# Start of a fused attention and MoE kernel: half of the first weight block in fp32, half cast on arrival, transposes moved, tiny loads dropped

## Chip, cores, metric

The kernel runs on one core of a Trainium2 chip. The metric is device time in microseconds (us) of one execution, lower is better. The time before the change is 219.72 us, the median of 5 runs (219.17 to 220.25).

## What is computed

The reference has two stages. The first is a two-way cross attention between `x` (8 batches, 8 heads, 512 rows, 64 wide) and `state` (8 batches, 8 heads, 32 rows, 64 wide). The second is a two-layer MLP with SiLU on all 4352 rows of its result.

```python
scores = scale * x @ state.T          # (B, H, 512, 32)
a      = softmax(scores)
xread  = a @ state                    # 512 rows per batch and head
a2     = softmax(scale * state @ x.T)
sread  = a2 @ x                       # 32 rows per batch and head
attn   = concat([xread, sread], axis=2)       # rows of 8 heads * 64 = 512
h      = attn @ w_in                  # 512 -> 2048
out    = (h * sigmoid(h)) @ w_out     # 2048 -> 512
```

## The kernel before, in words

The work goes batch by batch. For a batch `b`, TensorE transposes `x` (`x_T`, line 140), multiplies by the state to get the scores (`sc`), ScalarE takes the exponential (`ex`), VectorE and GpSimd normalise (`red`, `rec`, `norm_m`, `norm_g`), and TensorE transposes the softmax weights (`a_T`, line 223) into the tile `aT`. The first MLP layer is not applied to `xread`: since `xread @ w_in` equals `a @ (state @ w_in)`, the kernel forms `W1 = state @ w_in` once per batch (`w1_m`, line 275, in four column blocks `j` of 512, with `w1_e` casting each block from PSUM into the tile `W1`). Then `g1(b, ft)` (line 313) multiplies a 128-column piece of `W1` by `aT` for two halves and ScalarE applies SiLU to the sum; `g2` (line 339) multiplies the result by `w_out`, and `G2(b, ft)` does so for the four row tiles of one `ft`. `sread_m`, `sread_n`, `sread_t` compute the `sread` rows. `st_T(b)` transposes the state of a batch into `sbd`, which `w1_m` uses as its stationary operand.

The whole order of every engine is written out by hand (a manual schedule). Until line 572 the start is one long list; from line 575 on, a table of steps (`plan`) places the work of the later batches between the `g2` matmuls. The change touches the start only.

In the start, before the change:

- SyncE (its queue of transfers) loads `x` of batch 0 in four pieces (line 378), the state of batch 1 (`st_f[1]`, line 379), the first column block of `w_in` in four fp32 pieces `w_f[:, kt]` (line 381), then a part of `w_out` as fp32 `wo_f` (line 437). ScalarE's queue loads `st_f[0]` and two tiny pieces `tch` (lines 375 and 376, 0.5 KB each), GpSimd's queue a third (line 383). The other weights and `x` of batches 1 and 2 are loaded through GpSimd's queue, some with a cast on the way (`load_wi`, `load_wo`, `load_x`).
- Matmuls on a tile of zeros (`warm`, line 365) stand in TensorE's order at several places; `warm(6, "o0", 512)` (line 477) is the last group ahead of the first weight block.
- The first block of `W1` of batch 0 comes from fp32 operands: `w1f_m` (line 290) multiplies the fp32 state `sbd_f` by the four pieces of `w_f` (8 matmuls). After it come half of the evictions (`w1_e`, 256 columns, both by ScalarE), then `a_T` with both halves copied by VectorE, then the other evictions (lines 478 to 481).
- The bf16 copy of that block in `w_in_sb`, which batch 1 needs, is made by VectorE in four casts, two ahead of `sread_n` and two after the cast of the state of batch 1 (lines 493 to 500).

Of the kernel before, what the change touches and what calls it, by code (L numbers as in the profile page):

```python
# [8 lines left out]
FP32 = mybir.dt.float32  # L9
# [10 lines left out]
def kernel(  # L20
# [8 lines left out]
    nc = tc.nc  # L29
    ds = bass.ds  # L30

    B, H, S, NS, D, DM, DF = 8, 8, 512, 32, 64, 512, 2048
    KT = 4
    SCALE = 0.125

    pers = ctx.enter_context(tc.tile_pool(name="pers", bufs=1))
# [3 lines left out]

    zeros = pers.tile([128, 512], BF16, name="zeros")
    ident = pers.tile([128, 128], BF16, name="ident")
    tch = [pers.tile([16, KT, 2], FP32, name=f"tch{i}") for i in range(3)]
    st_f = [pers.tile([128, 128], FP32, name=f"st_f{i}") for i in range(2)]
    w_f = pers.tile([128, KT, 512], FP32, name="w_f")
    wo_f = pers.tile([128, 4, DM], FP32, name="wo_f")
    sbd_f = pers.tile([128, KT, NS], FP32, name="sbd_f")
# [16 lines left out]
    w_in_sb = pers.tile([128, KT, DF], BF16, name="w_in_sb")  # L64
# [3 lines left out]
    bank = {  # L68
        n: psum.tile([128, 512], FP32, name=f"ps_{n}")
        for n in ("o0", "o1", "w0", "w1", "h0", "h1", "a0", "a1")  # L70
    }
# [3 lines left out]
    win_re = moe_w_in.rearrange("(kt p) f -> p kt f", p=128)  # L75
    wout_re = moe_w_out.rearrange("(ft p) m -> p ft m", p=128)

    def bf(name):
        return bank[name][:].bitcast(BF16)

    def cp(eng, dst, src):
        if eng == "dve":
            nc.vector.tensor_copy(dst, src)  # L83
        elif eng == "pool":
            nc.gpsimd.tensor_copy(dst, src)  # L85
        else:
            nc.scalar.activation(dst, src, func=COPY, bias=0.0)  # L87
# [33 lines left out]
    def st_T(b, bk, e0, e1):  # L121
        v = bf(bk)[:, 0:128]
        nc.tensor.transpose(v, st_nat[:, b, :], ident[:])
        for half, e in ((0, e0), (1, e1)):
            cp(
                e,
                sbd[ds(64 * half, 64), b, :, half, :],
                v[ds(64 * half, 64)].rearrange("p (ns kt) -> p kt ns", kt=KT),
            )
# [93 lines left out]
    def a_T(b, bks):  # L223
        n = 2 // len(bks)
        for i, (bk, e) in enumerate(bks):
            v = bf(bk).rearrange("p (h c t) -> p h c t", h=2, c=4)
            for half in range(n):
                for c in range(4):
                    nc.tensor.transpose(
                        v[:, half, c, :], an[b % 2][:, i * n + half, c, :, :], ident[:]  # L230
                    )
            cp(e, aT[b % 2][:, ds(i * n, n)], v[:, ds(0, n)])
# [32 lines left out]
    def sread_t(b, bk, eng):  # L265
        v = bf(bk)[:, 512:640]
        nc.tensor.transpose(v, sr[:], ident[:])
        cp(
            eng,
            xsT[:, :, b // 4, :, b % 4],  # L270
            v.rearrange("p (kt ns) -> p kt ns", kt=KT),
        )


    def w1_m(b, j, bks):
        for kt in range(KT):
            for half in range(2):
                nc.tensor.matmul(  # L278
                    bank[bks[half]][ds(32 * kt, 32), :],
                    sbd[ds(64 * half, 64), b, kt, half, :],  # L280
                    w_in_sb[ds(64 * half, 64), kt, ds(512 * j, 512)],
                    start=True,
                    stop=True,
                    skip_group_check=True,
                    tile_position=(64 * half, 32 * kt),
                )

    def w1f_m(bks):  # L290
        for kt in range(KT):
            for half in range(2):
                nc.tensor.matmul(  # L293
                    bank[bks[half]][ds(32 * kt, 32), :],
                    sbd_f[ds(64 * half, 64), kt, :],
                    w_f[ds(64 * half, 64), kt, :],
                    start=True,
                    stop=True,
                    skip_group_check=True,
                    tile_position=(64 * half, 32 * kt),  # L300
                )

    def w1_e(b, j, bks, engs, c0=0, n=512):
        for half in range(2):
            cp(
                engs[half],
                W1[b % 2][:, half, ds(512 * j + c0, n)],
                bank[bks[half]][:, ds(c0, n)],
            )
# [3 lines left out]
    def g1(b, ft):  # L313
        bk = bank[f"h{hctr[0] % 2}"]
        hctr[0] += 1
        if b < B:
            for half in range(2):
                nc.tensor.matmul(  # L318
                    bk[:],
                    W1[b % 2][:, half, ds(128 * ft, 128)],  # L320
                    aT[b % 2][:, half, :, :],
                    start=(half == 0),
                    stop=(half == 1),
                    skip_group_check=True,
                )
            nc.scalar.activation(g[b % 2][:, ft, :], bk[:], func=SILU, bias=0.0)  # L326
        else:
            for kt in range(KT):
                nc.tensor.matmul(  # L329
                    bk[:, 0:256],  # L330
                    w_in_sb[:, kt, ds(128 * ft, 128)],
                    xsT[:, kt, :, :, :],
                    start=(kt == 0),
                    stop=(kt == KT - 1),
                    skip_group_check=True,
                )
            nc.scalar.activation(g_s[:, ft, :], bk[:, 0:256], func=SILU, bias=0.0)  # L337

    def g2(b, tt, ft, bk, cols=(0, 512)):
        src = g[b % 2] if b < B else g_s  # L340
        c0, c1 = cols
        nc.tensor.matmul(  # L342
            bank[bk][:, c0:c1],
            src[:, ft, ds(128 * tt, 128)],
            w_out_sb[:, ft, c0:c1],
            start=(ft == 0),
            stop=(ft == 15),
            skip_group_check=True,
        )
# [15 lines left out]
    def warm(n, bk, w=128):  # L365
        for i in range(n):
            nc.tensor.matmul(  # L367
                bank[bk][:, 0:w], zeros[:, 0:128], zeros[:, 0:w], start=True, stop=True,
                skip_group_check=True,
            )  # L370

    with tc.manual_schedule():

        nc.scalar.dma_start(st_f[0][:], state[0].rearrange("h ns d -> ns h d"))
        nc.scalar.dma_start(tch[0][:], win_re[0:128:8, :, 0:2])
        nc.scalar.dma_start(tch[1][:], wout_re[0:128:8, 0:4, 0:2])
        for kt in range(KT):
            load_x(0, nc.sync, kt, 1)
        nc.sync.dma_start(st_f[1][:], state[1].rearrange("h ns d -> ns h d"))
        for kt in range(KT):  # L380
            nc.sync.dma_start(w_f[:, kt, :], win_re[:, kt, 0:512])
        make_identity(nc, ident[:])
        nc.gpsimd.dma_start(tch[2][:], win_re[0:128:8, :, 512:514])
        nc.vector.memset(zeros[:], 0.0)
        nc.vector.memset(sbd[:], 0.0)
        for i in range(2):
# [12 lines left out]
        def G2(b, ft):  # L399
            for tt in range(4):  # L400
                g2(b, tt, ft, OB[tt])

        def W1x(b, j, bks, engs):
            w1_m(b, j, bks)
            w1_e(b, j, bks, engs)
# [68 lines left out]
        for i in range(4):  # L474
            cp("pool", w_out_sb[:, i, :], wo_f[:, i, :])
        nc.scalar.preload_act_table(SILU)
        warm(6, "o0", 512)
        w1f_m(("w0", "w1"))
        w1_e(0, 0, ("w0", "w1"), ("act", "act"), 0, 256)
        a_T(0, (("a0", "dve"), ("a1", "dve")))  # L480
        w1_e(0, 0, ("w0", "w1"), ("act", "dve"), 256, 256)
        warm(2, "h1", 512)
        load_x(1, nc.gpsimd, 2, 2)
# [12 lines left out]
        cp("dve", st_nat[:, 1, :], st_f[1][:])  # L496
        g1(0, 2)
        g1(0, 3)
        for kt in range(2, 4):
            cp("dve", w_in_sb[:, kt, 0:512], w_f[:, kt, :])  # L500
        st_T(1, "a0", "dve", "dve")
        G2(0, 0)
        sread_t(0, "a1", "dve")
        G2(0, 1)
        w1_m(1, 0, AB)
        W1x(0, 1, HB, DA)
        w1_e(1, 0, AB, DA)
        G2(0, 2)
        g1(0, 4)
        G2(0, 3)  # L510
        g1(0, 5)
        W1x(1, 1, AB, DD)
        G2(0, 4)
# [80 lines left out]
        def tiled(b, tt):  # L594
            cur, nxt, third, srb = (TB[(tt + i) % 4] for i in range(4))
            bks = ((nxt, third), HB, AB, (cur, srb))
            sread_m(b, srb)
            sread_n(b, srb)
            for j in range(4):
                w1_m(b, j, bks[j])  # L600
            for j in range(4):
                w1_e(b, j, bks[j], ("act", "dve"))
# [93 lines left out]
```

## Time and profile before

| what | value |
|---|---|
| median of 5 runs | 219.72 us (219.17 to 220.25) |
| the profiled execution's own time | 219.44 us |
| its span (first to last instruction) | 217.6 us |
| TensorE matmul busy | 211.2 us, 97% of the span |
| ScalarE, VectorE, GpSimd busy | 134.3 us (62%), 84.6 us (39%), 45.5 us (21%) |
| granted clock of TensorE | 1.000 (mean of the core) |

The span leaves 1.84 us around it (219.44 less 217.6). The busy share of TensorE is an average, and its records overlap because matmuls are pipelined, so a full slice can still hold waits. In the views, a line begins with the start in us and the duration in us, then the engine, the line of the kernel, the operation, the tiles as out<-in, shapes, and in brackets the idle time of the engine ahead of it with what ended it. PE is TensorE's matmuls, PEld its weight loads, DVE VectorE, ACT ScalarE, POOL GpSimd, SPq the transfers that SyncE issues.

### The profile page before, as it was taken

Reading aid. Unit: us, or ns where it says so; the run is one execution under the profiler, and the core shown is the slowest. Engines: PE = TensorE matmul, PEld = TensorE weight load, DVE = VectorE, ACT = ScalarE, POOL = GpSimd, SP = SyncE. Lnnn points to the kernel's source line nnn. Section 1 sums busy time; section 2 is a strip of 40 time slices with the busy share of each in tenths; the row PEclk is TensorE's granted clock in tenths of the full one; section 3 lists DMA queues with packets and bytes.
Section 4 is the critical chain, followed back from the end, with each engine's and each line's share of the span. In section 5 each row is a group of like instructions: output and inputs, shape, how many; then the busy total and the mean of one; then the engine's idle time right before and its main releaser. Section 6 shows DMA issues by size and latency. Waiting matters only on the chain.

```text
span 217.6 us, 4108 instructions
## 1 busy us (share of the span) xinstructions
PE 211.2 (97%) x1664; PEld 104.6 (48%) x1664; DVE 84.6 (39%) x176; ACT 134.3 (62%) x225; POOL 45.5 (21%) x87
## 2 busy tenths in 40 slices
PE   7989999999999999999999999999999999999993
PEld 7633454454444444444444444544454444566553
DVE  3765537832930463147313840276017501111110
ACT  3753485679767947884789458855885586233211
POOL 4596209300700070016001600070001000000000
PEclk9999999999999999999999999999999999999999
DMA  6999995696394149317831695146012311111112
GB/s 184 288 266 257 245 267 90 46 270 210 73 219 166 51 112 246 128 48 122 203 111 50 93 214 179 51 115 148 29 48 42 107 48 48 51 48 48 48 51 96
DMA packets 37555, 27.86 MB, mean 128 GB/s; under 512 B 22176, under 2 KB 31776, under 8 KB 37536
## 3 DMA queue, kind: packets, MB, share of 16 engines
q1 hardware_dynamic: 31280, 21.63, 37.5%
q0 software_dynamic: 5392, 5.44, 12.8%
q10 hardware_dynamic: 864, 0.53, 0.8%
q8 instruction: 13, 0.21, 0.4%
q14 instruction: 6, 0.05, 0.1%
HBM read 17.30 MB, written 8.91 MB: 120 GB/s over the span
## 4 chain that ended last, share of the span: by engine, by line
PE 94%; DVE 3%; ACT 1%; issue 0%; DVEq 0%; ACTq 0%
PE ps_o L342 28%; PE ps_w L342 26%; PE ps_h L318 25%; PE ps_h L329 3%; PE ps_o L367 2%; PE ps_a L175 2%; PE ps_a L278 1%; PE ps_w L293 1%; DVE w_in_sb L83 1%; PE ps_o L278 1%; PE ps_w L278 1%; PE ps_h L278 1%; DVE W L83 1%; PE ps_o L245 1%; DVE xT L83 1%; PE ps_o L143 0%
## 5 line engine op out<-in xcount | busy, mean ns | idle before, releaser
L326 ACT ACTIVATE g<-ps_h 128x512 bf16<-128x512 f32 x128 | 76.0, 597 | 36.6 <-PE ps_h L318 29.9
L318 PE MATMUL ps_h<-aT,W 128*128 128x512 bf16 x256 | 75.8, 379 | 0.2 <-DVE W L83 0.2
L342 PEld LDWEIGHTS <-g 128*128 128x128 bf16 x512 | 49.0, 98 | 54.9 <-issue 2.5
L342 PE MATMUL ps_w<-w_out_sb,g 128*128 128x512 bf16 x256 | 73.3, 379 | 0.0
L342 PE MATMUL ps_o<-w_out_sb,g 128*128 128x512 bf16 x256 | 65.9, 379 | 0.2
L318 PEld LDWEIGHTS <-W 128*128 128x128 bf16 x256 | 24.1, 98 | 28.1 <-issue 1.6
L201 POOL TENSOR_TENSOR an<-en,rs 128x512 bf16<-128x512 bf16 x8 | 8.4, 1054 | 112.3 <-ACT en L186 73.1
L83 DVE COPY o_sb<-ps_w 128x512 f32<-128x512 f32 (+1 forms) x13 | 8.5, 659 | 53.1 <-PE ps_w L342 53.0
L83 DVE COPY o_sb<-ps_o 128x512 f32<-128x512 f32 x14 | 9.5, 686 | 29.6 <-PE ps_o L342 29.5
L85 POOL CAST x_u<-x_f 128x256 bf16<-128x256 f32 x44 | 18.0, 454 | 0.0
L196 DVE TENSOR_REDUCE rs<-en 128x16 f32<-128x512 bf16 x14 | 9.2, 660 | 15.4 <-ACT en L186 15.3
L337 ACT ACTIVATE g_s<-ps_h 128x256 bf16<-128x256 f32 x16 | 6.1, 383 | 14.0 <-PE ps_h L329 14.0
L329 PE MATMUL ps_h<-xsT,w_in_sb 128*128 128x256 bf16 x64 | 9.6, 273 | 0.0
L83 DVE CAST W<-ps_a 128x512 bf16<-128x512 f32 x12 | 8.1, 682 | 3.7 <-PE ps_a L278 3.7
L87 ACT ACTIVATE o_sb<-ps_o 128x512 f32<-128x512 f32 (+1 forms) x4 | 2.2, 544 | 10.7 <-PE ps_o L342 7.9
L186 ACT ACTIVATE en<-ps_a 128x512 bf16<-128x512 f32 (+1 forms) x16 | 8.3, 568 | 0.5 <-PE ps_a L175 0.5
L329 PEld LDWEIGHTS <-w_in_sb 128*128 128x128 bf16 x64 | 6.3, 98 | 4.1
L175 PEld LDWEIGHTS <-xT 128*128 128x128 bf16 x128 | 6.0, 99 | 4.0 <-DVE xT L83 1.0
L186 ACT ACT_TABLE_LOAD x6 | 7.7, 1283 | 0.1
L609 ACT ACT_TABLE_LOAD x6 | 7.7, 1283 | 0.1
L87 ACT ACTIVATE o_sb<-ps_w 128x512 f32<-128x512 f32 (+1 forms) x5 | 2.7, 533 | 8.2 <-issue 6.6
L175 PE MATMUL ps_a<-sbd,xT 128*128 128x64 bf16 x120 | 6.1, 193 | 0.6 <-DVE xT L83 0.6
(87 smaller groups left out, 169.1 us busy)
## 6 DMA issues: line engine op xcount, KB each, us to landing
out_dram<-o_sb SPq DMA_DIRECT2D x32, 256.0 KB, 2.7
x_f<-in_x_dram SPq DMA_DIRECT2D x5, 1024.0 KB, 6.9
w_in_sb<-in_moe_w_in_dram POOLq DMA_DIRECT2D x3, 512.0 KB, 9.6
w_out_sb<-in_moe_w_out_dram POOLq DMA_DIRECT2D x3, 512.0 KB, 10.0
x_f<-in_x_dram SPq DMA_DIRECT2D x4, 256.0 KB, 3.9
w_f<-in_moe_w_in_dram SPq DMA_DIRECT2D x4, 256.0 KB, 5.4
wo_f<-in_moe_w_out_dram SPq DMA_DIRECT2D x4, 256.0 KB, 6.1
x_f<-in_x_dram POOLq DMA_DIRECT2D x2, 512.0 KB, 9.4
```

The lines of the kernel that those rows point to most:

```text
L83: nc.vector.tensor_copy(dst, src)
L85: nc.gpsimd.tensor_copy(dst, src)
L175: nc.tensor.matmul(v[:, kt % 2, :, c, :], xT[b % 2][:, kt, c, :], sbd[:, b, kt, :, :], start=True, stop=True, skip_group_check=True,)
L186: nc.scalar.activation(en[b % 2][:, :, :, ds(kt, n), :].rearrange("p h c k s -> p k (h c) s"), v[:, ds(kt % 2, n)], func=EXP, bias=0.0, sc ...
L196: nc.vector.tensor_reduce(v, en[b % 2][:, :, :, ds(kt, n), :], axis=AX, op=ADD)
L201: e.tensor_tensor(an[b % 2][:, ds(h0, hn), :, ds(kt, n), :].rearrange("p h c k s -> p (h c) k s"), en[b % 2][:, ds(h0, hn), :, ds(kt, n), ...
L278: nc.tensor.matmul(bank[bks[half]][ds(32 * kt, 32), :], sbd[ds(64 * half, 64), b, kt, half, :], w_in_sb[ds(64 * half, 64), kt, ds(512 * j, ...
L318: nc.tensor.matmul(bk[:], W1[b % 2][:, half, ds(128 * ft, 128)], aT[b % 2][:, half, :, :], start=(half == 0), stop=(half == 1), skip_group ...
L326: nc.scalar.activation(g[b % 2][:, ft, :], bk[:], func=SILU, bias=0.0)
L329: nc.tensor.matmul(bk[:, 0:256], w_in_sb[:, kt, ds(128 * ft, 128)], xsT[:, kt, :, :, :], start=(kt == 0), stop=(kt == KT - 1), skip_group_ ...
L342: nc.tensor.matmul(bank[bk][:, c0:c1], src[:, ft, ds(128 * tt, 128)], w_out_sb[:, ft, c0:c1], start=(ft == 0), stop=(ft == 15), skip_group ...
L609: nc.scalar.preload_act_table(SILU)
```

## The change

The three tiny loads and their tiles go. `w1f_m` takes one `kt` and is called for `kt` 0 and 1 only. For `kt` 2 the piece `w_f` is cast to bf16 by ScalarE, for `kt` 3 by VectorE, and `w1_m`, which now takes a list of `kt`, does these two from the bf16 tile. `a_T` stands ahead of those two, and its second half is copied by ScalarE instead of VectorE. The evictions of the first 256 columns are split between ScalarE and VectorE. Five of six zero matmuls ahead of the block go. The later casts of `kt` 2 and 3 go. `G2(0, 2)` moves ahead of the blocks `w1_m(1, 0)` and `W1x(0, 1)`, and `G2(0, 3)` ahead of `g1(0, 4)`.

```diff
-    tch = [pers.tile([16, KT, 2], FP32, name=f"tch{i}") for i in range(3)]
-    def w1_m(b, j, bks):
-        for kt in range(KT):
+    def w1_m(b, j, bks, kts=range(KT)):
+        for kt in kts:
...
-    def w1f_m(bks):
-        for kt in range(KT):
-            for half in range(2):
+    def w1f_m(bks, kt):
+        for half in range(2):
...
         nc.scalar.dma_start(st_f[0][:], state[0].rearrange("h ns d -> ns h d"))
-        nc.scalar.dma_start(tch[0][:], win_re[0:128:8, :, 0:2])
-        nc.scalar.dma_start(tch[1][:], wout_re[0:128:8, 0:4, 0:2])
...
         make_identity(nc, ident[:])
-        nc.gpsimd.dma_start(tch[2][:], win_re[0:128:8, :, 512:514])
...
         nc.scalar.preload_act_table(SILU)
-        warm(6, "o0", 512)
-        w1f_m(("w0", "w1"))
-        w1_e(0, 0, ("w0", "w1"), ("act", "act"), 0, 256)
-        a_T(0, (("a0", "dve"), ("a1", "dve")))
+        warm(1, "o0", 512)
+        w1f_m(("w0", "w1"), 0)
+        w1f_m(("w0", "w1"), 1)
+        cp("act", w_in_sb[:, 2, 0:512], w_f[:, 2, :])
+        cp("dve", w_in_sb[:, 3, 0:512], w_f[:, 3, :])
+        a_T(0, (("a0", "dve"), ("a1", "act")))
+        w1_m(0, 0, ("w0", "w1"), (2, 3))
+        w1_e(0, 0, ("w0", "w1"), ("act", "dve"), 0, 256)
         w1_e(0, 0, ("w0", "w1"), ("act", "dve"), 256, 256)
         warm(2, "h1", 512)
...
         g1(0, 2)
         g1(0, 3)
-        for kt in range(2, 4):
-            cp("dve", w_in_sb[:, kt, 0:512], w_f[:, kt, :])
         st_T(1, "a0", "dve", "dve")
         G2(0, 0)
         sread_t(0, "a1", "dve")
         G2(0, 1)
+        G2(0, 2)
         w1_m(1, 0, AB)
         W1x(0, 1, HB, DA)
         w1_e(1, 0, AB, DA)
-        G2(0, 2)
+        G2(0, 3)
         g1(0, 4)
-        G2(0, 3)
         g1(0, 5)
```

More of the change, by code (lines that the diff above doesn't have):

```diff
@@ L286, in w1_m @@
                 )
-    def w1f_m(bks):
-        for kt in range(KT):
-            for half in range(2):
[L293 to L301, printed above, removed]
+    def w1f_m(bks, kt):
+        for half in range(2):
+            nc.tensor.matmul(
+                bank[bks[half]][ds(32 * kt, 32), :],
+                sbd_f[ds(64 * half, 64), kt, :],
+                w_f[ds(64 * half, 64), kt, :],
+                start=True,
+                stop=True,
+                skip_group_check=True,
+                tile_position=(64 * half, 32 * kt),
+            )
     def w1_e(b, j, bks, engs, c0=0, n=512):
```

## The prediction

> **What bounds the kernel now.** I read the page's chain of work first, then the chain over the first 27 us, then the order of time around it. All times are us from the span's start.
>
> ```profile
> PE 94%; DVE 3%; ACT 1%; issue 0%; DVEq 0%; ACTq 0%
> ```
>
> TensorE sets the end: its chain is 94% of the span and the change takes no needed matmul away. From 16.42 on the chain is nearly all matmuls, so the question is how much earlier the steady part can begin, and whether it stays earlier. The chain's window shows what delays it:
>
> ```profile
> 8.93 1.29 PE ps_o L367 x6
> 10.23 1.98 PE ps_w L293 x16
> 12.20 0.34 PE ps_a L229 x4
> 12.54 0.02 issue
> 12.57 0.76 DVE aT L83 x2
> 13.32 0.33 DVE W L83
> 13.65 1.93 DVE w_in_sb L83 x2
> 15.59 0.09 DVE srec L257
> 15.67 0.02 issue
> 15.70 0.29 DVE sr L258
> 15.99 0.16 DVE st_nat L83
> 16.14 0.05 issue
> 16.19 0.23 PE ps_a L123
> 16.42 0.43 PE ps_w L342 x2
> ```
>
> Six zero matmuls fill a wait, then the fp32 matmuls; then for 3.6 us (12.57 to 16.19) the chain runs over VectorE: copies of aT, one W eviction, two weight casts, sread_n, the cast of the next state. Only then come st_T (16.19) and the first g2 (16.42). The order of time shows why the fp32 matmuls end at 12.20:
>
> ```profile
> 10.47 0.14 PEld L293 LDWEIGHTS ps_w<-w_f,sbd_f 64*32 64x32 f32 x4 [0.16 <-DMA w_f<-in_moe_w_in_dram]
> 11.15 0.14 PEld L293 LDWEIGHTS ps_w<-w_f,sbd_f 64*32 64x32 f32 x4 [0.54 <-DMA w_f<-in_moe_w_in_dram]
> 11.15 1.05 PE L293 MATMUL ps_w<-w_f,sbd_f 64*32 64x512 f32 x4
> ```
>
> The last weight piece lands just ahead of 11.15, and the last kt then costs 1.05. So the arrival of w_f[3], not the zero matmuls, sets this point: taking away 5 x 0.215 = 1.08 us of zero matmuls is worth nothing by itself.
>
> **The change, part by part.**
>
> *From the last piece to the first g1.* Now: 11.15, fp32 to 12.20, transposes to 12.54, aT copies to 13.32; the first g1 starts at 13.04 and its SiLU at 13.79. Changed: the piece is cast by VectorE, which is free (its norm_g ends 10.76). For that cast I have these rows:
>
> ```profile
> 13.57 1.26 DVE L83 CAST w_in_sb<-w_f 128x512 bf16<-128x512 f32 x1
> 16.05 0.41 DVE L83 CAST w_in_sb<-w_f 128x512 bf16<-128x512 f32 x1
> 16.39 0.61 DVE L83 CAST w_in_sb<-w_f 128x512 bf16<-128x512 f32 x1
> ```
>
> The long one starts while GpSimd casts wo_f (from 13.36); the short two run beside a load that GpSimd issues (16.00 to 16.77). At 11.15 GpSimd also issues a load (load_wo(1), 11.07 to 11.87), so the short rows are nearest: I take 0.5, bounds 0.41 and 1.26. [...]
>
> So: cast to 11.65; w1_m for kt 3 at 11.70, ending at 12.10 (x8 of that shape took 0.41); evictions side by side on ScalarE (0.38 for 256 columns) and VectorE (0.41) to 12.5; first g1 about 12.55, its second half 12.77, first SiLU 13.17 instead of 13.79. The rest lies beside this: ScalarE's cast of kt 2 follows the table load (ends 10.65), 0.6 by its other 512-wide copies, to 11.25. The softmax weights are complete at 11.12 (GpSimd's norm_g, 10.37 + 0.75), the transposes end about 11.5, ScalarE's copy of the second half (0.60, row of xT) ends 12.1. That ties with the W path, so if w_f came sooner, g1 could gain only 0.07 more. Gain here 0.62.
>
> *From g1 to st_T.* g1(0,2) and g1(0,3) each wait for the SiLU that frees their PSUM bank, so they move by 0.62 as well; TensorE is free of them at about 14.7. VectorE has the second W eviction to 12.86, then only the two casts of kt 0 and 1. The first starts before GpSimd's casts begin at 13.36 (0.5), the second beside them (0.8, as 14.76 to 15.59 in the trace): 14.3. Then srec to the end of the state's cast, 0.64 as now (15.51 to 16.14): 14.95, st_T at 14.98 instead of 16.19: 1.21 earlier. Bounds: with both casts at 1.26 it is 16.1 (gain 0.1); with both at 0.41 TensorE's own 14.7 decides (gain 1.5). The two later casts (1.0 of VectorE at 16.05) hid behind nothing that TensorE waited for after 16.19 and count zero.
>
> *The moved g2 blocks.* Their matmuls are the same number. G2(0,2) now lies where TensorE waits for sbd and xsT of batch 1: in the trace w1_m starts 0.09 after the last g2 matmul could end, so this gives 0 to 0.1. G2(0,2) needs the third cast of wo_f (about 15.3, needed at 16.9) and SiLU 2. Two g1 now stand together, and G2(0,4) has only g1(0,5) and w1_m(1,1) (0.43 + 0.34) to hide SiLU 4 (0.16 + 0.60): a stall of 0 to 0.1. I set the two against each other: 0.
>
> *The tiny loads.* ScalarE's two issues (0.61, 0.44) end ahead of the table load, which ends at 3.91, while the next instruction waits for st_f until 4.07; GpSimd's issue (0.71) ends at 2.22 and its next work waits for x until 3.87. Their issue is hidden: 0. SyncE's queue changes more: in the built order each load waits on the one eight before it, and w_f[2] (5.01) and wo_f[0] (6.22) waited on tiny loads (1.51 + 3.5, 2.15 + 4.1). Without them w_f goes out from 3.57 on instead of 4.06, so 0.5 to 0.6 earlier. But the transfer engines are 93 to 105% busy from 2 to 12, and the queue is in order behind x and st_f, so I take 0 for the landing. Bounds: 0.6 earlier, worth up to 0.3 at st_T (TensorE's 14.7); 1.8 later if the tiny loads prepared something (a 0.5 KB load took 3.5 to 4.1, a 32 KB st_nat load 2.3).
>
> *Does it last?* What could take it back are transfers through GpSimd's queue, whose issue does not move: w_in block 1 lands at 16.33 (7.33 + 9.0), used from 18.0; w_out 1 at 18.9, used 20.5; w_in 2 at 21.5, used 23.3; x of batch 1 at 23.0 and 24.4, whose casts now end near 25.6 at the latest against transposes then at 26.2 (27.47 less 1.2); w_in 3 at 29.4, used 31.5; w_out 3 at 31.9, used 34.4; x of batch 2 at 34.9, used 37.0. All land in time, the tightest with 0.6. After that every load is issued behind work that moves along, and the tail is one unbroken g2 run.
>
> **Sum.** 1.21 + 0 + 0 = 1.2. 219.44 - 1.2 = 218.24 against the profiled execution; that execution was 0.28 below the median of the runs, against which it is 218.52. I forecast 218.4.
>
> **The rivals.**
>
> *Casts blocked.* GpSimd holds VectorE up at 11.15 (0.75 more than 0.5) or at both later casts. For it: the 1.26 row. Against: the 0.41 row. W, g1 and st_T come 0.7 later than forecast: 219.1. Chance 0.20.
>
> *Earlier arrival.* w_f lands up to 0.6 sooner and x slightly too, without the 0.5 KB packets. st_T at TensorE's limit: gain 1.5 to 1.7, 217.9. Chance 0.08.
>
> *TensorE's clock drops* (the other side). The zero matmuls gone, TensorE works with gaps between 9.15 and 12.1: by the steps above some 0.6 us there are without matmul, in four pieces of at most 0.4. The rows: the 128x128 zero matmuls average 313 ns in the window 1 to 4.5 and 222 ns in 6.3 to 7, so the array is slow until about 6.1, some 4.9 us after its first matmul. If it fell back at 12.5 and took that long again, 4.9 us would hold half of its work: 2.4 lost, 1.2 gained, 220.6. It turns slower once slow speed lasts over 2.4 us. Against: the trace keeps speed over the 0.67 idle ahead of 16.19. Chance 0.06. [...]
>
> *The tiny loads mattered.* Then w_f lands up to 1.8 later, 219.44 + 1.8 - 1.2 = 220.0; slower from 1.2 on. Against: st_nat, first reads of state in mid-kernel, lands in 2.3. Chance 0.06.
>
> *The start moves and nothing follows* (a later wait absorbs it): 219.4 to 219.7, chance 0.02.
>
> **How the numbers follow.** Forecast 0.58. A difference under 0.3% (0.66 us) is about what a measurement of this kernel can't tell from none. Faster: 0.58 + 0.08 = 0.66. Same: 0.20 + 0.02 = 0.22. Slower: 0.12. The range leaves out the two slower rivals and a little more: 217.6 (gain 1.7 from the profiled time with 0.1 for spread) to 219.6.
>
> **What would show it.** Right: the first SiLU near 13.2, st_T near 15.0, the first g2 near 15.1, the cast of w_f[3] near 0.5, and the chain from there all TensorE with the same gap to the end. Wrong: that cast above 1 us, w_f landing later than 11.15, 128-wide matmuls near 313 ns after 9, or a new wait on w_out, x of batch 1 or SiLU 4 after 16.

## The result, and the profile after

The changed kernel takes 218.73 us (median of 44 runs, 217.71 to 220.02) where the kernel before takes 219.48 us beside it (79 runs, 218.4 to 220.67). The ratio is 0.9967 (95% interval 0.9958 to 0.9977): 0.72 us gained, 0.5 to 0.9. The forecast was 1.2 us, a time of 218.4 with a range of 217.6 to 219.6. The time lies in the range and the sign is right; the gain is some six tenths of the forecast one. That it lies in the range says little by itself: the range's upper end, 219.6, is above the 219.48 of the kernel before.

The profiled execution of the changed kernel took 218.28 us with a span of 216.5 us, so against the profiled execution before (219.44 and 217.6) it shows 1.16 us. That is more than the medians show, and the difference is the main lesson of this case.

The page's chain of work, by engine:

```profile
PE 93%; DVE 4%; ACT 1%; issue 1%; DVEq 0%; ACTq 0%
```

The end is still TensorE's. The chain over the first 27 us (start, duration, engine, tile, line):

```profile
10.87 0.62 PE ps_a L228 x8
11.49 0.69 PE ps_w L277 x4
12.17 0.02 issue
12.20 0.76 DVE W L82 x2
12.95 1.14 DVE w_in_sb L82 x2
14.09 0.33 issue
14.43 0.16 DVE srec L256
14.59 0.02 issue
14.61 0.29 DVE sr L257
14.90 0.21 DVE st_nat L82
15.12 0.05 issue
15.16 0.23 PE ps_a L122
15.39 0.43 PE ps_w L338 x2
```

It is the shape of the chain before, without the fp32 matmuls at its head. The transposes (line 228) now run at 10.87, ahead of the last weight piece; the bf16 pair of kt 2 and 3 follows; then VectorE holds the chain from 12.20 to 15.12. The next state's transpose stands at 15.16 (16.19 before, forecast 14.98) and the first g2 of the chain at 15.39 (16.42 before). The order of time has the rows on which the forecast leaned most:

```profile
11.04 0.97 POOL L105 DMA_DIRECT2D w_out_sb<-in_moe_w_out_dram  x1
...
11.27 0.43 DVE L82 CAST w_in_sb<-w_f 128x512 bf16<-128x512 f32 x1 [0.55 <-DMA w_f<-in_moe_w_in_dram]
...
12.87 0.89 DVE L82 CAST w_in_sb<-w_f 128x512 bf16<-128x512 f32 x1
...
13.24 1.08 ACT L322 ACTIVATE g<-ps_h 128x512 bf16<-128x512 f32 x2 [0.42 <-PE ps_h L314]
...
13.68 0.82 DVE L82 CAST w_in_sb<-w_f 128x512 bf16<-128x512 f32 x1
```

The first cast, on arrival, took 0.43 (forecast 0.5). The other two took 0.89 and 0.82 where I had 0.5 and 0.8. The first SiLU began at 13.24 (forecast 13.17).

### The profile page after: what moved, and what is told of

The parts are those of the page before. It is cut to its first block, busy times and chain, and to the rows that moved or that the text cites. A ratio compares the mean times of both kernels' runs of the same rounds, so it can differ in the third digit from the quotient of the medians.

```text
span 216.5 us, 4086 instructions
## 1 busy us (share of the span) xinstructions
PE 210.1 (97%) x1655; PEld 104.5 (48%) x1655; DVE 84.1 (39%) x175; ACT 135.2 (62%) x226; POOL 45.4 (21%) x86
## 4 chain that ended last, share of the span: by engine, by line
PE 93%; DVE 4%; ACT 1%; issue 1%; DVEq 0%; ACTq 0%
PE ps_o L338 28%; PE ps_w L338 27%; PE ps_h L314 25%; PE ps_h L325 3%; PE ps_o L363 2%; PE ps_a L174 1%; PE ps_a L277 1%; PE ps_w L277 1%; DVE W L82 1%; PE ps_o L277 1%; PE ps_h L277 1%; DVE xT L82 1%; PE ps_o L244 1%; DVE rs L437 1%; DVE w_in_sb L82 1%
## 5 line engine op out<-in xcount | busy, mean ns | idle before, releaser
L82 DVE CAST W<-ps_h 128x512 bf16<-128x512 f32 x9 | 6.1, 682 | 2.2 <-PE ps_h L277 2.2
```

## The experiments

In each comparison the kernel before ran on the same chip. Every profile gives three moments that I follow through all runs: A, the start of the work that waits for the last weight piece (the last fp32 pair in the old form, VectorE's cast of kt 3 in the new); B, the first SiLU; C, st_T, the transpose of the state of batch 1. "Casts" is the time of VectorE's two weight casts that lie between B and C.

### The tiny loads

The kernel before without them:

```diff
-        nc.scalar.dma_start(tch[0][:], win_re[0:128:8, :, 0:2])
-        nc.scalar.dma_start(tch[1][:], wout_re[0:128:8, 0:4, 0:2])
...
-        nc.gpsimd.dma_start(tch[2][:], win_re[0:128:8, :, 512:514])
```

> The kernel before, only without its three tiny loads. My theory (the gain comes from the path between the last weight piece and the first g2, and the tiny loads cost and give nothing): no difference, ratio 0.998 to 1.002; SyncE issues w_f about 0.5 us earlier but the last piece still lands near 11.15, the first SiLU near 13.8, st_T near 16.2. Rival (the loads of w_f go out earlier and therefore land earlier): last piece near 10.6, st_T near 15.7, ratio 0.9975. Rival (the tiny loads prepared the weights' loading): last piece later than 11.7 and ratio over 1.002.

Measured: ratio 1.0008 (0.9987 to 1.0029). A is 11.27 (11.15 before) and B 13.90. The other way round, the changed kernel with the tiny loads put back:

> The changed kernel, only with the three tiny loads put back. My theory: the same as the changed kernel, ratio to before 0.9945 to 0.9985, with the cast of the last weight piece starting near 11.2 and st_T near 15.2. Rival (the tiny loads' absence is what gains): ratio back to 0.999 to 1.001 and the last piece 0.5 us later than in the changed kernel.

Measured: ratio 0.9966 (0.9942 to 0.9990), the same as the changed kernel; A is 11.15. Within these intervals the tiny loads neither helped nor hurt, and the earlier issue of w_f (from 3.60 on in the changed kernel, from 4.06 on in the kernel before) did not bring the last piece sooner.

### The zero matmuls

The kernel before with one instead of six:

```diff
-        warm(6, "o0", 512)
+        warm(1, "o0", 512)
```

> The kernel before, only with one zero matmul of 512 columns instead of six ahead of the first weight block. My theory: the block's end is set by the last weight piece (11.15), so no difference: ratio 0.998 to 1.002, the first fp32 matmul near 9.1 to 9.4 instead of 10.16, the last pair still at 11.15 and the first SiLU near 13.8. Rival (the zero matmuls delay the block): first SiLU up to 0.5 us earlier, ratio near 0.9975. Rival (they keep the clock up): matmuls of 512 columns start 0.43 us apart instead of 0.22 somewhere after 9, ratio 1.004 or more.

Measured: ratio 0.9990 (0.9968 to 1.0011). All four fp32 pairs now wait for their pieces (9.41, 10.11, 10.76, 11.44), and B follows A by 2.64 as before. No gain shows from the removal alone. The changed kernel with six:

> The changed kernel with six zero matmuls instead of one. My theory: now that only kt 0 and 1 stand ahead of the transposes, the zero matmuls would be in the way: fp32 from about 10.1 on, ending near 11.1 to 11.3 instead of 10.3, transposes near 11.0 to 11.3 instead of 10.87, first SiLU 0.1 to 0.5 us later, ratio to before 0.997 to 0.9995. Rival (TensorE's clock suffers without them in some executions and widens the spread): ratio at or under 0.9967 and a smaller spread than the changed kernel's 217.71 to 220.02.

Measured: ratio 0.9977 (0.9954 to 1.0000), median 218.96 beside 218.63 for the changed kernel in the same comparison. The intervals overlap, and in the profile the last piece came late (A 11.87), so that the delayed fp32 pairs (10.11 and 10.54) were hidden behind it. Whether the five zero matmuls cost something in the changed order stays open. The spread is 217.98 to 219.72 with them and 217.98 to 219.97 for the changed kernel beside them, 12 runs each: too near to tell.

### VectorE's order

The changed kernel, with the state's cast moved into VectorE's idle time and one weight cast moved behind sread_n:

```diff
+        cp("dve", st_nat[:, 1, :], st_f[1][:])
         cp("dve", w_in_sb[:, 3, 0:512], w_f[:, 3, :])
...
-        for kt in range(2):
-            cp("dve", w_in_sb[:, kt, 0:512], w_f[:, kt, :])
+        cp("dve", w_in_sb[:, 0, 0:512], w_f[:, 0, :])
         sread_n(0, "a1")
-        cp("dve", st_nat[:, 1, :], st_f[1][:])
+        cp("dve", w_in_sb[:, 1, 0:512], w_f[:, 1, :])
```

> The changed kernel with VectorE's order changed: the cast of the state of batch 1 moved ahead of the cast of the last weight piece (VectorE idles there, 10.73 to 11.27 in the changed kernel), and the cast of the weight piece kt 1 moved behind sread_n. My theory (st_T at 15.16 waits for VectorE's two weight casts, 0.89 and 0.82, where I had forecast 0.5 and 0.8): st_T moves to the end of g1(0,3), about 14.8 to 14.95, 0.2 to 0.35 us earlier than in the changed kernel, ratio to before near 0.995. Rival (TensorE or SiLU sets st_T already): st_T stays within 0.1 of 15.16 and the ratio stays at 0.9967. Rival (sbd and xsT, now behind the moved cast, hold up w1_m of batch 1): a wait on VectorE ahead of w1_m after 16.5 takes the gain back.

Measured: ratio 0.9938 (0.9918 to 0.9958), median 217.92; the theory asked for a ratio near 0.995, which lies in the interval. The changed kernel with the tiny loads, beside it in the same comparison, has a median of 218.65. The profiled execution was a late one (218.73): A was 11.99. Its order of time:

```profile
11.99 0.43 DVE L82 CAST w_in_sb<-w_f 128x512 bf16<-128x512 f32 x1 [1.26 <-DMA w_f<-in_moe_w_in_dram]
...
12.47 0.39 PE L277 MATMUL ps_w<-w_in_sb,sbd 64*32 64x512 bf16 x2 [1.10 <-DVE w_in_sb L82]
...
13.32 1.04 PE L314 MATMUL ps_h<-aT,W 128*128 128x512 bf16 x4
...
14.86 0.17 DVE L256 RECIPROCAL srec<-ps_a 128x2 f32<-128x2 f32 x1 [0.51 <-PE ps_a L244]
```

VectorE now waits for TensorE (0.51 ahead of the reciprocal), not TensorE for VectorE, and C comes 1.57 after B. That is what SiLU and g1(0,3) need: the chain of this profile from B to C holds only ScalarE's SiLU and TensorE. Also, TensorE idled 1.10 us here ahead of 12.47, yet its four matmuls at 13.32 took 1.04 together, the time of the same group in the changed kernel.

The same idea in the kernel before, with the old fp32 block (and the new places of the g2 blocks):

```diff
-        for kt in range(2):
-            cp("dve", w_in_sb[:, kt, 0:512], w_f[:, kt, :])
+        cp("dve", st_nat[:, 1, :], st_f[1][:])
+        cp("dve", w_in_sb[:, 0, 0:512], w_f[:, 0, :])
         sread_n(0, "a1")
-        cp("dve", st_nat[:, 1, :], st_f[1][:])
+        cp("dve", w_in_sb[:, 1, 0:512], w_f[:, 1, :])
...
+        st_T(1, "a0", "dve", "dve")
         for kt in range(2, 4):
             cp("dve", w_in_sb[:, kt, 0:512], w_f[:, kt, :])
-        st_T(1, "a0", "dve", "dve")
```

> The kernel before with the order of VectorE and of the g2 blocks alone changed: the cast of the state of batch 1 ahead of the weight casts, one cast ahead of sread_n and one behind, the other two behind st_T; G2(0,2) ahead of w1_m of batch 1 as in the change. The first weight block stays all fp32, the zero and tiny matters stay. My theory of two bounds in series (arrival and fp32 until the first SiLU at 13.79, then VectorE's chain until st_T at 16.19): the first SiLU stays at 13.8, st_T comes when g1(0,3) is done, 15.4 to 15.6, so 0.6 to 0.8 us earlier, ratio near 0.9968, as much as the whole change. Rival (all of the gain hangs on the first block of W1): st_T gains under 0.2 us or a wait on the late casts ahead of w1_m takes it back, ratio 0.999 to 1.001.

Measured: ratio 0.9978 (0.9958 to 0.9998), median 218.88. From B to C it is 1.56, and A to B stays 2.64 (11.87 to 14.51). So with the whole first block left as it was, the order of VectorE and of the g2 blocks is worth about 0.5 us by the ratio (0.04 to 0.9). That is less than the 0.6 to 0.8 that the theory asked for; the next experiment finds nothing for the g2 places.

### The places of the g2 blocks

The changed kernel with G2(0,2) and G2(0,3) where they were:

> The changed kernel with the old places of G2(0,2) and G2(0,3). My theory: the two small stalls offset each other, ratio to before 0.995 to 0.9985, the chain's gain after 20 us within 0.15 of the changed kernel's. Rival (w1_m of batch 1, now needed near 17.2, waits for the load of w_in block 1 or for xsT): a wait of 0.3 us or more ahead of it, ratio 0.998 to 1.000.

Measured: ratio 0.9965 (0.9947 to 0.9983). From C to the second copy of xT at 28.67 it is 12.87 us, in the changed kernel also 12.87 (15.16 to 28.03). The two places are worth nothing, as forecast. This profile has the longest weight casts of all, and beside them, on GpSimd, the casts of wo_f without a pause. Its order of time:

```profile
12.89 1.56 DVE L82 CAST w_in_sb<-w_f 128x512 bf16<-128x512 f32 x1
...
12.97 1.19 POOL L84 CAST w_out_sb<-wo_f 128x512 bf16<-128x512 f32 x2
...
14.08 1.59 POOL L84 CAST w_out_sb<-wo_f 128x512 bf16<-128x512 f32 x2
...
14.37 0.83 DVE L82 CAST w_in_sb<-w_f 128x512 bf16<-128x512 f32 x1
```

In the kernel before without tiny loads the same two VectorE casts took 0.45 and 0.41; there GpSimd was waiting for a piece of wo_f from 13.85 to 14.21 (order of time):

```profile
13.69 0.45 DVE L82 CAST w_in_sb<-w_f 128x512 bf16<-128x512 f32 x1
...
14.06 0.41 DVE L82 CAST w_in_sb<-w_f 128x512 bf16<-128x512 f32 x1
...
14.21 0.73 POOL L84 CAST w_out_sb<-wo_f 128x512 bf16<-128x512 f32 x1 [0.36 <-DMA wo_f<-in_moe_w_out_dram]
```

### Second profiles of both kernels

> The changed kernel once more, for a second profile. The two profiles so far differ by 1.1 us in span and 1.16 us in time, the medians by 0.75. My theory: the difference is the spread of single executions, which arises in the first 13 us (arrival of x and w_f and the moment at which TensorE's clock rises); this profile shows another st_T time than 15.16, and its distance to that equals the difference of the spans within 0.2 us. Rival: the start is the same and the spans differ by something later.

Measured: ratio 0.9974 (0.9950 to 0.9998). The profiled execution took 218.66, span 216.8 us, A 11.53, C 15.43. C is 0.27 later than in the first profile, the span 0.3 longer: the difference arises in the start. B is 1.97 after A again, C 1.93 after B.

> The kernel before once more, for a second profile. My theory: from the last weight piece to the first SiLU 2.64 us again (2.64, 2.63, 2.64, 2.64 in four profiles with the old first block), while the time from the first SiLU to st_T, 2.40 in the first profile, is another (1.57 and 1.94 in the two that only lack tiny loads or zero matmuls), with the length of VectorE's two casts (2.01, 0.79, 1.55) to explain it. Rival: 2.40 again, so that the changed kernel's 1.92 to 2.04 is a saving to be counted.

Measured: ratio 1.0001 (0.9980 to 1.0022). A is 11.64, B 14.28 (2.64 again), C 15.99: 1.71 after B, not 2.40. The casts took 1.00:

```profile
14.06 1.00 DVE L83 CAST w_in_sb<-w_f 128x512 bf16<-128x512 f32 x2
```

The saving that I had read from the first profile's 2.40 was one draw, a length that another execution of the same kernel does not have.

### Without GpSimd's casts

```diff
+        nc.gpsimd.memset(w_out_sb[:, 0:4, :], 0.0)
...
-        for i in range(4):
-            cp("pool", w_out_sb[:, i, :], wo_f[:, i, :])
```

> The changed kernel without GpSimd's four casts of the first quarter of w_out (wo_f): those rows of w_out are zeros, set once at the start while GpSimd waits for x, so a quarter of the second layer's sum is left out; TensorE does the same matmuls. GpSimd's later loads go out some 2.6 us earlier. My theory (after the first SiLU, st_T waits for VectorE's two weight casts, which GpSimd's casts hold up for 0.4 to 1.5 us, so what the change saves ahead of the first SiLU is partly lost there, differently in each execution): from the first SiLU to st_T 1.55 to 1.75 instead of 1.92 to 2.54, the two casts 0.8 to 1.0 together, median 0.3 to 0.7 us under the changed kernel's, ratio to before 0.9935 to 0.996. Rival (the casts are slow by themselves or held up by the loads that GpSimd issues): the two casts still take 1.5 or more, ratio 0.9965 to 0.998.

This kernel leaves out a quarter of the second layer's sum, and GpSimd's later loads go out earlier in it (the load of w_out issued at 16.82 in the changed kernel is issued at 13.88), so its time is not that of the casts alone.

Measured: median 218.19, ratio 0.9949 (0.9924 to 0.9973), in the range that the theory gave, though the interval overlaps that of the changed kernel; the two casts took 0.94. But in its profile B to C was 1.95, a miss, and no shorter than the changed kernel's 1.92 and 1.93: VectorE waited 0.33 for sread_m, and then the state's small cast, 0.23 in the kernel before, took 0.58 beside a load that GpSimd issued (order of time):

```profile
14.62 0.77 POOL L100 DMA_DIRECT2D w_in_sb<-in_moe_w_in_dram  x1
...
14.86 0.58 DVE L82 CAST st_nat<-st_f 128x128 bf16<-128x128 f32 x1
```

So it isn't GpSimd's casts alone: a load that it issues can go with a long VectorE cast too.

### Two faster versions

The kernel with VectorE's new order, with the state of batch 1 loaded behind w_f and cast after the W evictions (VectorE's order as in the diff on the kernel before, above):

```diff
-        nc.sync.dma_start(st_f[1][:], state[1].rearrange("h ns d -> ns h d"))
         for kt in range(KT):
             nc.sync.dma_start(w_f[:, kt, :], win_re[:, kt, 0:512])
+        nc.sync.dma_start(st_f[1][:], state[1].rearrange("h ns d -> ns h d"))
```

> The kernel of the VectorE order experiment (cast of kt 1 behind sread_n), with the load of the state of batch 1 moved behind the four loads of w_f in SyncE's queue and its cast placed after the W evictions. My theory: what varies most is the arrival of the last w_f piece (11.15 to 11.99 in the profiles so far); with 64 KB of small packets behind it instead of ahead, it lands 0.2 to 0.3 us sooner, median 217.6 to 217.8, ratio to before 0.992 to 0.9935. Rival (the transfer engines interleave and the arrival does not move, or the softmax weights at 10.4 to 11.3 take over as the bound): median within 0.15 of 217.92, ratio 0.9935 to 0.9945. Rival (the state now lands late and its cast holds VectorE): slower than 218.1.

Measured: median 217.94, ratio 0.9939 (0.9916 to 0.9961): the rival's numbers. A was 11.16, and C, at 14.85, was the earliest of all, but GpSimd's third cast of wo_f waited until 16.25 for its piece, and G2(0,2) began at 16.91, where G2(0,1), begun at 15.83 and 0.86 long, would have let it begin near 16.70. In the order of time:

```profile
16.25 0.61 POOL L84 CAST w_out_sb<-wo_f 128x512 bf16<-128x512 f32 x1 [2.06 <-DMA wo_f<-in_moe_w_out_dram]
```

With the old places of the g2 blocks on top:

> The kernel with the VectorE order and the state of batch 1 loaded behind w_f, and with the old places of G2(0,2) and G2(0,3). In the profile without this last edit G2(0,2) waited 0.2 us (to 16.91) for GpSimd's cast of the third piece of wo_f, which landed at 16.25. My theory (the next bound is the arrival of the w_out pieces, and w_m of batch 1 can fill that wait): no wait on GpSimd's cast in the chain before 18, 0.1 to 0.25 us sooner, median 217.7 to 217.85, ratio 0.9920 to 0.9935. Rival (w1_m of batch 1, needed near 16.7, then waits for xsT or for w_in block 1 instead): ratio 0.9935 to 0.995 with a wait ahead of w1_m.

Measured: median 217.86 (5 runs), ratio 0.9916 (0.9898 to 0.9933), the best ratio of the study; its chain before 18 has no wait on GpSimd. Its A was 11.87, so the later state load does not bring the last piece forward reliably; its part in the gain is not shown. In both kernels the last piece was asked for at 4.26 and 4.28, 0.9 sooner than in the changed kernel (5.18), and it was there at 11.16 and 11.87, against 11.27: asking earlier did not make it land earlier. Both versions beat the kernel before, and both have lower ratios than the changed kernel, but only the last one's interval lies clear under the changed kernel's 0.9958 to 0.9977. Between the three with VectorE's new order and the new first block the intervals overlap.

## Why the prediction was right or wrong

The moments from all profiles of the start (us). "Split" stands where the two casts do not follow each other; the last column is C less B. Below, "the four old-order profiles" are the first four rows, and "the five changed kernels" are the sixth to the tenth.

| kernel | A | B less A | casts | C less B |
|---|---|---|---|---|
| before | 11.15 | 2.64 | 2.01 | 2.40 |
| before, second profile | 11.64 | 2.64 | 1.00 | 1.71 |
| before, no tiny loads | 11.27 | 2.63 | 0.79 | 1.57 |
| before, one zero matmul | 11.44 | 2.64 | 1.55 | 1.94 |
| before, VectorE's order | 11.87 | 2.64 | split | 1.56 |
| changed | 11.27 | 1.97 | 1.64 | 1.92 |
| changed, second profile | 11.53 | 1.97 | 1.70 | 1.93 |
| changed, tiny loads back | 11.15 | 2.24 | 1.18 | 2.04 |
| changed, old g2 places | 11.19 | 2.07 | 2.31 | 2.54 |
| changed, six zero matmuls | 11.87 | 1.97 | 1.54 | 1.77 |
| changed, VectorE's order | 11.99 | 1.97 | split | 1.57 |
| changed, no wo_f casts | 11.57 | 1.97 | 0.94 | 1.95 |
| changed, VectorE's order, state later | 11.16 | 2.13 | split | 1.56 |
| the same, old g2 places | 11.87 | 1.97 | split | 1.57 |

**What bounds the kernel: right.** Removing zero matmuls alone gives nothing that can be measured: the fp32 pairs then wait for their pieces, and the last piece sets the block's end.

**From the last piece to the first SiLU: right.** Forecast 0.62. B less A falls from 2.64 to 1.97 where the cast on arrival takes 0.43, and to 2.07 and 2.24 where it takes 0.53 and 0.69; over the five changed kernels 2.04 on average, 0.59 saved. The 0.41 and 0.61 rows were near what that cast took. No run separates the parts of this step (bf16 for two pieces, the earlier transposes, the copies and evictions shared out between two engines).

**From the first SiLU to st_T: wrong.** The forecast gave this stretch 0.59 (2.40 down to 1.81), from "two casts, 0.5 and 0.8" against 2.01. Its own terms add up to less than it wrote: 12.86, 0.5 and 0.8 make 14.16, not 14.3, so they would have promised 0.14 more. Both ends were mis-sized. The five changed kernels have 2.04 on average (casts 1.67 on average, not 1.3). And the 2.40 of the profile before was a late draw: the four kernels with the old order average 1.91, with casts from 0.79 to 2.01. On average the stretch gained nothing: it is 0.13 longer, which single values from 1.57 to 2.54 do not tell from zero. I took the duration of one such cast, saw it vary threefold among four casts of one profile (0.41 to 1.26), used that for the new casts' bounds, and did not ask whether the old sum of 2.01 was itself typical.

**Sum.** 0.59 from A to B, -0.13 from B to C and 0.07 from A itself (11.47 on average in the five profiles with the old first block, 11.40 in the five changed kernels) make 0.53. The 0.07 is chance: all nine profiles with the new first block average 11.51, and arrival varies from 11.15 to 11.99 whatever the kernel. From C to VectorE's last copy it is 197.94 on average in the four old-order profiles and 197.80 in the five changed kernels, another 0.14 gained. Together 0.67, against 0.72 measured by the ratio. The averages are over four or five executions each, so this is a sum that fits, not a proof of each term.

Most of the 0.14 lies at one place far behind the start, at the first g1 of batch 4, near 104 us. It reads the softmax weights of that batch (`aT`), which a transfer transposes. In the first profile before, that transfer lands 4.9 us after its issue at 98.75, and the g1 starts as it lands, at 103.66; in the changed kernel it lands after 3.1 and nothing waits for it. Up to there the SiLUs of the first profile before are 1.03 behind those of the changed kernel, from there on 1.22, so 0.19 of the 1.16 us between the two profiled executions lies there. The other old-order profiles lose 0.07, 0.11 and nothing at this place (landing after 4.7, 4.8 and 3.1), the five changed kernels at most 0.03. The most, 0.60, is lost in the kernel before with VectorE's order, where the profile names a wait of 0.44:

```profile
103.96 0.59 PE L318 MATMUL ps_h<-aT,W 128*128 128x512 bf16 x2 [0.44 <-DMA aT<-an]
```

The slow landing comes in four of the five profiles with the old first block and in one of the nine with the new one. No run shows why, nor whether the change has a part in it; the prediction has no such term, so for the forecast this share of the gain is luck.

**Tiny loads, g2 places: right at zero.** Both ways round for the tiny loads; 12.87 against 12.87 for the places. SiLU 4 brought no stall: the g2 run of the chain at 20.85 follows w1_m at once.

**It lasts: right.** No transfer took the gain back: C to the second copy of xT is 12.87 in both profiles of the changed kernel and 12.87 to 12.99 in the four old-order ones.

**The rivals.** "Casts blocked" was the nearest, in its second form: not the cast on arrival but the later two, which are as long in the kernel before, within the scatter. The measured 218.73 lies between the forecast 218.4 and this rival's 219.1. "Earlier arrival" did not come: the last piece was there at 11.27 and 11.53, not ahead of 11.15. The clock rival found no support: the eight 128-wide transposes after 10 us took 0.62 together before and after the change, with starts 0.057 apart on average. The 30 zero matmuls of that width from 1.19 on, which the forecast calls slow, took 3.38 together in both kernels, with starts 0.106 apart: about half the pace. The granted clock reads 1.00 over both stretches, so the views show a change of pace and not of the clock. Nor did the rival that the tiny loads mattered.

**VectorE's casts beside GpSimd.** The cast at 11.27 ran beside a load that GpSimd issued: VectorE took 0.43, and GpSimd's issue took 0.97, where the issue after it took 0.75. In the other profiles with the new first block this cast took 0.43 to 0.69. Of the casts between B and C, two took 0.45 and 0.41 mostly while GpSimd waited (before, no tiny loads), and one 1.56 while it cast without a pause (changed, old g2 places). The runs show this pattern; none shows its cause.

## What to carry to other kernels

A duration that differs from one execution to the next (here 2.01 and 1.00 us for the same two casts of the kernel before) is a draw, on the removed side of the sum as on the added one; compare the stretch in several executions before counting it as a saving. Where two bounds stand in series, cutting the first only shows the second: here moving two casts on VectorE took the ratio from 0.9967 (0.9958 to 0.9977) to 0.9938 (0.9918 to 0.9958). Put a cast that needs only old data into an idle time of its engine, not into the stretch that the next stage waits for.

## What the runs showed that I had not expected

One and the same pair of casts (128x512, fp32 to bf16, VectorE) took 0.79 to 2.31 us in the profiles, and the last weight piece was there from 11.15 to 11.99, with no visible tie to the moment at which it was asked for (4.26 to 6.19). How much of the 2.3 us between the fastest and the slowest execution of the changed kernel each explains was not separated; the 12 runs with the casts off that stretch lay between 217.53 and 218.73.
